# A transformer block on one core: the beginning dealt by a list schedule, with another form of the modulation

## The chip, the cores and the metric

The kernel runs on one core of a Trainium2 chip. The metric is the device time of one execution in microseconds (us). The engines are called as in the profile: PE is the matrix engine (PEld its weight loads), DVE the vector engine (VectorE), ACT the scalar engine, POOL is GpSimd, SP the engine that issues most loads and stores. Each runs its own queue in order; semaphores join them.

## What is computed

One block on x of 2048 tokens and 512 columns, all in float32: a modulated normalization, sliding-window attention of 32 heads with a window of 256, a gated residual, a second modulated normalization, a gated feed-forward part with 1792 inner columns, and a gated residual. All six modulation rows come from one vector c. Of the reference:

```python
mod = (_silu(c) @ w_mod).reshape(c.shape[0], 6, 1, -1)
sa, ca, ga, sb, cb, gb = (mod[:, 0], mod[:, 1], mod[:, 2], mod[:, 3], mod[:, 4], mod[:, 5])
h = _layernorm(x, axis=-1) * (1 + ca) + sa
x = x + ga * _A_ref(h, A_wqkv, A_wo)
h = _layernorm(x, axis=-1) * (1 + cb) + sb
x = x + gb * _B_ref(h, B_w1, B_w3, B_w2)
```

## The kernel before

Tokens are worked in four blocks of 512, each of four tiles of 128; the 512 columns are four quarters of 128. A float32 operand of a product is split into a high part, rounded to the fast matmul type (fp32r), and a low part; a product of two such operands is three matmuls.

The program has three phases. The **beginning** (all that this change touches) does this for each block: load four tiles of x, take mean and variance (`ln_tile`, L376 and L377), the root on POOL (L371), normalize on DVE (`ln_apply`, L381), then for each column quarter transpose four tiles on PE (L687), scale and shift on ACT with the modulation of that quarter (L388), split into high part (cast, L390) and low part (subtraction, L391), both on DVE. The result is `hT`. From it PE makes the values, twelve matmuls for each of 16 tiles (`values`, L709), evicted by ACT into `vS`, and, for the first group of heads, the queries and keys of blocks 0 to 2, twelve matmuls each (`unit_a`, L489). These are evicted three times by ACT (L495 to L501), two differences are made on POOL (`mix`, L507), and six loads lay them out in `ring`, whose constant rows POOL fills by memset (`ring_fill`, L460 to L463). For blocks 0 and 1 `unit_b` also runs the 16 score matmuls (L542) with the row maximum of each on DVE (L549). The weights of the values are split into `wvh` (ACT, L665) and `wvl` (L668: quarter 0 on POOL, the other three on DVE).

The **modulation** has six rows: for the first norm, j = 0 (shift) and 1 (scale); gates 2 and 5; for the second norm 3 and 4. Each row is loaded as four blocks of 256 KB into `stage`, which lies in the not yet used part of `vS`. PE multiplies silu(c), repeated over 32 columns, by the four blocks in four column groups of its array at once (L628), ACT evicts (L634), and a second set of matmuls sums the groups and turns the row into columns (L642) or, for the gates, into a row (L639) that is stored in `g_dr` and read much later.

The **middle** runs the attention of all other units by a table of times (`X`), and the **end** (second half of the attention's output, feed-forward) is dealt by `Sched`, a list schedule: operations with engine, price, key (the time wished), tiles read and written and PSUM banks are taken in the order in which a model clock frees their engine. Neither is touched.

In the beginning the order is written by hand: each operation is put down with a time by `at(t, fn)` with offsets from the table `W`, the whole list is sorted, and each engine's queue is that list, filtered. The values of a block are put down so that they run behind, among the transposes and projections of the block after it.

Of the kernel before, what the change touches and what calls it, by code (L numbers as in the profile page):

```python
# [8 lines left out]
F32 = mybir.dt.float32  # L9
# [34 lines left out]
W = dict(m=0.15, s=0.1, a=0.29, t=0.541, p=0.377, vs=1.762, vo=0.422, wq=(-1.8, 1.47, 1.5), wv0=-1.811, wvh=(-0.7, -0.65, -0.6, -0.55), wvl=(-0.5, -0.31, -0.3, -0.25), wp=1, A0=2.1, h0=0.539, h=6, hb=6.874, ls=3.287, la=1.146, rf=(1.55, 1.56, 8.4), v=2, vt=1.75, mr=(-1.85, 1.55), mm=(2.6, 4.625, 5.85, 9.2), ml=(-1.79, 1.25, 2.0, 4.9), A=1.268, At=7.876, B=10.4)  # L44
# [70 lines left out]
class Sched:  # L115
    def __init__(self, banks, take, fixed, urgent):


        self.ops, self.last, self.readers = [], {}, {}
        self.banks, self.take, self.fixed, self.urgent, self.tag = banks, take, fixed, urgent, None  # L120
        Bank.made = {}
# [33 lines left out]
    def deal(self):  # L155
# [20 lines left out]
        while left:  # L176
            best = None
            for e, lst in ready.items():
                t, pick = free[e], None
                for key, seq, o in lst:  # L180
# [10 lines left out]
                    if o.kb:  # L191

                        b = max(s, t)
                        end = max(wire, b + 1.5) + o.kb / RATE + o.more
                        s = max([s] + [u + 0.01 for u in self.urgent if b <= u < end])
                    if s <= t + (LOOK[e] if o.att else 0.0):
                        pick = (max(s, t), o)
                        break
# [35 lines left out]
            if o.kb:  # L234
                s = max(s, lanes.pop(0))
                wire = max(wire, s + 1.5) + o.kb / RATE + o.more
                o.lat = wire + LATE - s
# [43 lines left out]
def us(t):  # L281
# [8 lines left out]
             side_probs=("ACT", 0.48), values=("PE", 0.66), cut_all=("ACT", 0.48), store=("SP", 0.45))  # L290
NPE = 3
# [32 lines left out]
def block_kernel(ctx: ExitStack, tc: tile.TileContext, x, wqk, wv, wo, w13, w2, c, wmod, out):  # L324
# [11 lines left out]
    o32 = cst.tile([P, P], F32, name="o32")  # L336
    nc.gpsimd.memset(o32, 1.0 / 32)
    odd = cst.tile([P, 1], F32, name="odd")

    def fill_odd():  # L340
# [6 lines left out]
        nc.vector.tensor_copy(identr, ident)  # L347

    modc = cst.tile([P, 4, KC], F32, name="modc")
    sc32 = cst.tile([P, KC, 32], F32, name="sc32")  # L350
# [15 lines left out]

    def rstd_of(pool, mv, n, tag):
        var = pool.tile([P, n], F32, name=tag + "v")
        nc.vector.tensor_scalar_add(var, mv[:, :n, 1], EPS)
        rs = pool.tile([P, n], F32, name=tag + "r")  # L370
        nc.gpsimd.tensor_tensor(out=rs, in0=var, in1=nhalf[:, :n], op=ALU.pow)  # L371
        return rs

    def ln_tile(pool, xin, mv, i):
        st = pool.tile([P, nc.vector.BN_STATS_DIM], F32, name="bst", bufs=4)
        nc.vector.bn_stats(st, xin)  # L376
        nc.vector.bn_aggr(mv[:, i], st)  # L377

    def ln_apply(pool, xin, mv, rs, i, tag):
        xn = pool.tile([P, D], F32, name=tag, bufs=4) if tag else xin  # L380
        nc.vector.tensor_scalar(xn, xin, mv[:, i, 0:1], rs[:, i:i + 1], op0=ALU.subtract,  # L381
                                op1=ALU.mult)
        return xn

    def mod_split(pool, hT, src, k, lo, at):

        h = pool.tile([P, BT], F32, name="h32", bufs=3)
        nc.scalar.activation(h, src, AF.Identity, bias=modc[:, at, k:k + 1],  # L388
                             scale=modc[:, at + 1, k:k + 1])
        nc.vector.tensor_copy(hT[:, 0, k, lo:lo + BT], h)  # L390
        nc.vector.tensor_tensor(out=hT[:, 1, k, lo:lo + BT], in0=h,  # L391
                                in1=hT.bitcast(F32)[:, 0, k, lo:lo + BT], op=ALU.subtract)

# [26 lines left out]
    nc.gpsimd.memset(vS[:, :4, :, DH:], 1.0)  # L420

# [9 lines left out]
    def keys(rows, hh, a, b, n):  # L431
# [4 lines left out]
    nc.gpsimd.memset(mskq, 0.0)  # L436
    nc.gpsimd.affine_select(out=mskq[:, :P], in_=mskq[:, :P], pattern=[[1, P]], base=0,
                            channel_multiplier=-1, compare_op=ALU.is_gt, fill=NEG)
    nc.gpsimd.affine_select(out=mskq[:, 2 * P:], in_=mskq[:, 2 * P:], pattern=[[-1, P]], base=0,
                            channel_multiplier=1, compare_op=ALU.is_ge, fill=NEG)  # L440
    mskw = a1.tile([P, KC, P], F32, name="wqr", bufs=1)
    mskk = mskw[:, :2]
    nc.gpsimd.memset(mskk, 0.0)
    WIN = (dict(pattern=[[1, P]], base=0, channel_multiplier=-1, compare_op=ALU.is_ge, fill=NEG),
           dict(pattern=[[-1, P]], base=0, channel_multiplier=1, compare_op=ALU.is_gt, fill=NEG))
    for j in range(2):
        nc.gpsimd.affine_select(out=mskk[:, j], in_=mskk[:, j], **WIN[j])
# [4 lines left out]
    def fill_masks():  # L452
        nc.vector.tensor_copy(mskr, mskw[:, :2])
        nc.vector.tensor_scalar(later, mskw[:, 0], 0.0, None, op0=ALU.is_lt)
# [3 lines left out]
    def ring_fill(b, hh):  # L458
        k = ring.bitcast(F32)[:, 2 - 2 * hh, :, b * BT:(b + 1) * BT]
        nc.gpsimd.memset(k[:NM] if hh == 0 else k[:NS], 0.0)  # L460
        if hh:
            nc.gpsimd.memset(k[NS:NM], 1.0)
        nc.gpsimd.memset(k[NS:NS + 2], 1.0 - hh)  # L463
# [16 lines left out]
    def unit_a(u, t0, at, y=X):  # L480
# [35 lines left out]

        if b == 1 and g + 1 < NQ:
            for n in range(3):
                at(t0 + y["wqk"][n], lambda n=n: load_wqk(g + 1, n))
        for n in range(3 * KC):  # L520
            at(t0 + y["pj"][n], lambda n=n: product(n), "product")
        for n in range(3):
            at(t0 + y["ev"][n], lambda n=n: out(n), "out")
        at(t0 + y["mix"][0], lambda: mix(1), "mix")
        at(t0 + y["mix"][1], lambda: mix(2), "mix")
        for r in range(3):
            at(t0 + y["row"][r], lambda r=r: rows(r), "qk_rows")
# [1166 lines left out]
```

## Time and profile before

| what | us |
|---|---|
| median of 3 runs | 966.52 (965.93 to 967.31) |
| the profiled execution | 965.88, its span 963.9 |
| PE busy in the span | 938.2 (97%) |
| DVE, ACT, POOL busy | 720.3, 552.2, 524.9 |
| first matmul of the beginning | at 7.46 |
| first value product | at 19.93 |
| last value product, first operation of the middle | at 95.57, at 95.81 |

A row of the timeline gives the start, the duration, the engine, the source line, the operation with output and input tiles, the shapes and the count; in brackets the engine's idle time just before it and what ended it. Matmuls overlap, so what one costs is read from the distance between starts. The table by stretch gives busy microseconds of PE, PEld, DVE, ACT and POOL, with counts, then the granted PE clock, the DMA share and GB/s.

### The profile page before, as it was taken

To read this page: it belongs to the slowest core of one execution; us is meant where nothing else is said; L and a number is where in the kernel's file an instruction comes from. 1 tells how busy PE (TensorE), PEld (TensorE's weight loads), DVE (VectorE), ACT (ScalarE), POOL (GpSimd) and SP (SyncE) were. 2 spreads that over 40 slices of the span, in tenths; PEclk is the share of its full clock that TensorE was granted. 3 is DMA by queue.
4 is the path that set the end of the run, shared out by engine and by line. 5 is a ranking of instruction groups with operands and counts; after the bars stand their busy time and mean duration, and the time that the engine had idled before them with its cause. 6 is when DMAs were issued, how large, how long until landed. Compare 5 with 4: busy or idle time off the path is not lost.

```text
span 963.9 us, 17134 instructions
## 1 busy us (share of the span) xinstructions
PE 938.2 (97%) x5316; PEld 717.5 (74%) x5316; DVE 720.3 (75%) x2041; ACT 552.2 (57%) x1258; POOL 524.9 (54%) x734
## 2 busy tenths in 40 slices
PE   6999999999999999997999999999999999999998
PEld 3678777677777776774788778888888888888886
DVE  7575899898989898998568695666679665566545
ACT  3333877787878787875768944433456333433330
POOL 8321787777777777765643865368457332221320
PEclk9999999999999999998899999999999999999999
DMA  9521354444454444337692664575554523222002
GB/s 314 177 78 57 108 176 157 137 154 144 145 177 144 145 145 145 134 127 219 194 283 86 226 206 151 185 262 175 185 179 165 169 78 99 60 73 78 30 23 87
DMA packets 81559, 141.64 MB, mean 147 GB/s; under 512 B 10554, under 2 KB 23226, under 8 KB 81468
## 3 DMA queue, kind: packets, MB, share of 16 engines
q1 hardware_dynamic: 80748, 139.50, 44.6%
q10 hardware_dynamic: 720, 1.05, 0.3%
q8 instruction: 42, 0.69, 0.3%
q14 instruction: 49, 0.40, 0.1%
HBM read 85.72 MB, written 34.61 MB: 125 GB/s over the span
## 4 chain that ended last, share of the span: by engine, by line
PE 86%; DVE 4%; POOL 4%; DMA 2%; issue 2%; ACT 1%; SPq 0%; POOLq 0%; DVEq 0%; ACTq 0%
PE st L1469 11%; PE mx L1469 11%; PE pj L489 7%; PE mx L542 7%; PE st L819 7%; PE po L780 7%; PE mx L1563 6%; PE st L1563 6%; PE po L1469 4%; PE st L709 4%; PE pj L1469 3%; PE po L1563 2%; PE mx L1205 2%; PE pj L1563 2%; POOL pt L847 2%
## 5 line engine op out<-in xcount | busy, mean ns | idle before, releaser
L549 DVE CUSTOM_DVE_ANT_0 junk<-mx,mskq 128x384 bf16<-128x384 f32 (+2 forms) x503 | 251.9, 527 | 28.9 <-PE mx L542 27.5
L542 PE MATMUL mx<-ring 96*128 96x384 f32 (+1 forms) x503 | 151.9, 340 | 3.8 <-DMA ring<-qk 1.3
L819 PE MATMUL st<-ring 100*128 100x384 f32 (+2 forms) x488 | 148.7, 346 | 0.5 <-ACT pt L840 0.4
L847 POOL TENSOR_SCALAR_AFFINE_SELECT pt<-pt 128x256 f32<-128x256 f32 x268 | 108.6, 408 | 64.6 <-ACT pt L840 54.2
L489 PE MATMUL pj<-hT,wq 128*128 128x512 f32 x384 | 135.9, 404 | 0.8 <-DVE wq L478 0.8
L542 PEld LDWEIGHTS mx<-ring 96*128 96x128 f32 x503 | 92.2, 189 | 35.5 <-DVE mt L549 23.2
L1513 POOL TENSOR_TENSOR t<-t,t 128x512 f32<-128x512 f32 x28 | 41.0, 1463 | 137.6 <-DVE t L1501 133.8
L840 ACT ACTIVATE pt<-st 128x256 f32<-128x256 f32 x263 | 94.3, 386 | 36.2 <-DVE st L837 28.1
L819 PEld LDWEIGHTS st<-ring 100*128 100x128 f32 x488 | 91.7, 191 | 18.8 <-issue 6.7
L780 PE MATMUL po<-pt,vS 128*17 128x256 f32 (+2 forms) x1408 | 97.9, 390 | 2.3 <-POOL pt L847 1.8
L507 POOL TENSOR_TENSOR qk<-qkr,qk 128x512 fp32r<-128x512 f32 x64 | 83.3, 1301 | 27.6 <-ACT qkr L495 27.4
L837 DVE COPY_PREDICATED st<-later,st 128x128 f32<-128x128 uint8 x263 | 71.0, 291 | 13.4 <-PE st L819 10.6
L489 PEld LDWEIGHTS pj<-hT,wq 128*128 128x128 f32 x384 | 71.4, 190 | 9.6 <-issue 1.7
L1060 POOL TENSOR_TENSOR w<-w,w 128x512 fp32r<-128x512 f32 (+2 forms) x35 | 55.5, 1602 | 34.0 <-PE pj L1563 17.8
L780 PEld LDWEIGHTS po<-pt,vS 128*17 128x17 f32 x1408 | 32.8, 97 | 47.1 <-issue 21.0
L1501 DVE TENSOR_TENSOR t<-mx,t 128x512 f32<-128x512 f32 x54 | 36.9, 687 | 36.9 <-PE mx L1469 34.0
L1469 PE MATMUL st<-b,w 128*128 128x512 f32 x240 | 60.2, 390 | 1.4 <-ACT t L1508 1.4
L864 POOL TENSOR_SCALAR_AFFINE_SELECT sm<-sm 128x256 f32<-128x256 f32 x109 | 41.9, 406 | 28.4 <-ACT sm L854 24.3
L1469 PE MATMUL mx<-b,w 128*128 128x512 f32 x228 | 57.0, 391 | 0.0
L831 ACT ACTIVATE pt<-st 128x384 f32<-128x384 f32 (+2 forms) x109 | 45.7, 434 | 14.0 <-DVE st L827 12.5
L1469 PEld LDWEIGHTS st<-b,w 128*128 128x128 f32 x240 | 45.0, 188 | 11.4 <-ACT t L1508 1.8
L1501 DVE TENSOR_TENSOR t<-st,t 128x512 f32<-128x512 f32 x35 | 24.1, 688 | 37.1 <-PE st L1469 33.3
(322 smaller groups left out, 2097.0 us busy)
## 6 DMA issues: line engine op xcount, KB each, us to landing
ring<-qk SPq DMA_DIRECT2D x192, 128.0 KB
o_dr<-os SPq DMA_DIRECT2D x32, 256.0 KB
w<-wsum SPq DMA_DIRECT2D x14, 512.0 KB
w<-w2g SPq DMA_DIRECT2D x14, 512.0 KB
jb<-in_w SPq DMA_DIRECT2D x24, 256.0 KB
wraw<-in_w SPq DMA_DIRECT2D x7, 768.0 KB
w<-wraw SPq DMA_DIRECT2D x14, 384.0 KB
vS<-in_wmod SPq DMA_DIRECT2D x20, 256.0 KB
```

Source lines behind the costliest of these rows:

```text
L489: nc.tensor.matmul(v["ps"], WQ[g][w][:, n // 3], hTp(i, n // 3, b * BT, BT), start=(n == 0), stop=(n == 3 * KC - 1))
L507: nc.gpsimd.tensor_tensor(out=v[n], in0=v["raw"], in1=v[1].bitcast(F32), op=ALU.subtract)
L542: nc.tensor.matmul(v[i][:, :n], queries(NS, a, gq, 1), keys(NS, hh, a, k0, gq + 1 - k0), start=True, stop=True)
L549: nc.vector.tensor_tensor_reduce(out=junk[:, :n], in0=v[i][:, :n], in1=mskq[:, 3 * P - n:], scale=1.0, scalar=-3e38, op0=ALU.add, op1=ALU. ...
L780: nc.tensor.matmul(po[32 * i:32 * i + DH + 1, qb * P:(qb + nq) * P], vS[:, kb, 4 * g + i], pts[i // 2][:, i % 2, c0:c0 + nq], start=first, ...
L819: nc.tensor.matmul(ps[:, :nq], keys(NM, hh, a, kb, 1), queries(NM, a, kb, nq), start=True, stop=not plus)
L837: nc.vector.copy_predicated(ps[:, 0], later, ps[:, 2])
L840: nc.scalar.activation(pt_of(j, a)[:, hh, :2], v[j, a, hh][:, :2], AF.Exp, scale=SCALE)
L847: nc.gpsimd.affine_select(out=pt[:, :, 2 * m], in_=pt[:, :, 0], **w)
L1469: nc.tensor.matmul(ps(bk), WT[s, n][w][:, col], BB[t, k][r], start=start and c == 0, stop=stop and c == 5, skip_group_check=True)
L1501: return nc.vector.tensor_add(o, x, y)
L1563: nc.tensor.matmul(ps(bk), tiles[hk + (h,)][:, i * P:(i + 1) * P], w2_of(last, y, f), start=(m == 0), stop=(m == 5))
```

## The change

The beginning is no longer put down by hand. Every operation of it is entered by `do` or `dma` with its engine, price, key and the tiles that it reads and writes; `unit_a` and `unit_b` enter theirs through `at`; and `Sched` deals them, with the tables `K0` and `W0` of keys, its own DMA rate (`RATE0`) and look-ahead (`LOOK0`). [...]

Further:
- **First norm's modulation** (j = 0, 1): the weights are stored by column quarters. A quarter's four 128x128 blocks are stationary and a column of silu(c) moves (`mod_rows`), so that shift and scale of a quarter come out as columns at once (`mod_out`). Loads are interleaved: shift, scale and value weights of one quarter after the other.
- **Second norm's** (j = 3, 4): transposed weights, multiplied on DVE by silu(c), which is broadcast to all partitions (`crep`), and summed along the row (`mod_cols`), eight passes.
- **Gates** (j = 2, 5): each as one row, four accumulating matmuls with one column of silu(c) stationary (`gate_row`).
- All four `wvl` are made on POOL; two of the four first x tiles are loaded from ACT's queue; x has six buffers, by name; memsets of `ring` and masks become single operations; five matmuls on zeros stand first on PE.

```diff
+K0 = dict(wv=(7.0, 8.5), wl=1.0, h0=11.0, hb=19.0, tn=3.0, st=8.0, ap=4.0, mj=(22.0, 24.0), mg=(24.0, 40.0), rf=(13.0, 23.0, 40.0, 60.0),
+          va=3.0, pj=1.5, B=6.0, off=OFF0)
+RATE0, LATE0 = 390.0, 0.6
...
-        self.ops, self.last, self.readers = [], {}, {}
+        self.ops, self.last, self.readers, self.rate, self.late, self.look = [], {}, {}, RATE, LATE, LOOK
...
+    def apply(t):
+        nc.vector.tensor_scalar(xt[t], xt[t], mv[:, t, 0:1], rs[:, t // 4, 1, t % 4:t % 4 + 1],
+                                op0=ALU.subtract, op1=ALU.mult)
...
+    def mod_rows(j, n, bk):
+        w = stage[:, KC + KC * j + n].rearrange("p (k c) -> p k c", c=P)
+        for k in range(KC):
+            nc.tensor.matmul(ps(bk)[:, 2 * n + j:2 * n + j + 1], w[:, k], sc[:, k:k + 1], start=(k == 0),
+                             stop=(k == KC - 1))
+
+    def mod_out(n, bk):
+        nc.vector.tensor_tensor(out=modc[:, 0:2, n], in0=ps(bk)[:, 2 * n:2 * n + 2], in1=plus, op=ALU.add)
+
+
+    def mod_cols(j, n, i):
+        nc.vector.tensor_tensor_reduce(out=stage[:, i], in0=stage[:, i], in1=crep, scale=1.0, scalar=0.0,
+                                       op0=ALU.mult, op1=ALU.add, accum_out=modc[:, 2 + j, n:n + 1])
...
+    def gate_row(j, k, i, bk):
+        nc.tensor.matmul(ps(bk)[:1], sc[:, k:k + 1], stage[:, i], start=(k == 0), stop=(k == KC - 1))
...
+    for n in range(5):
+        bk = Bank("at")
+        do(0.5 + 0.1 * n, "PE", lambda bk=bk: nc.tensor.matmul(ps(bk)[:4], zero[:, 0], zero[:, 0, 0:1].to_broadcast([P, BT]),
+                                                                  start=True, stop=True), [], [bk], 0.46)
...
+        do(K0["wv"][1] + 2 * n, "POOL", lambda n=n: nc.gpsimd.tensor_tensor(
+            out=wvl[:, n], in0=stage[:, n], in1=wvh.bitcast(F32)[:, n], op=ALU.subtract), [("stg", n), ("wvh", n)],
+            [("wvl", n)], 1.24)
...
+        for n in range(5):
+            do(K0["rf"][b] + 1.0 * n, "POOL", lambda b=b, n=n: ring_fill(b, n), [], [("fill", b)], 1.0, port=False)
...
+            do(h - K0["ap"] + 0.46 * i + 0.5, "DVE", lambda t=t: apply(t), [q, ("rs", b)], [q], 0.46)
...
+            do(h - K0["tn"] + 1.3 * k + 1.5, "PE", lambda b=b, k=k, bk=bk: turn(b, k, bk), [
+                ("xt", (4 * b + i) % XS) for i in range(4)], [bk], 0.50)
+            do(h - K0["tn"] + 1.3 * k + 2.0, "ACT", lambda b=b, k=k, bk=bk: shifted(b, k, bk), [bk, ("mod", k)], [s_], 0.66)
+            do(h - K0["tn"] + 1.3 * k + 2.7, "DVE", lambda b=b, k=k: part(b, k, 0), [s_], [("hT", b, k, 0)], 0.46)
+            do(h - K0["tn"] + 1.3 * k + 3.2, "DVE", lambda b=b, k=k: part(b, k, 1), [s_, ("hT", b, k, 0)],
+               [("hT", b, k, 1)], 0.61, port=True)
...
+            do(K0["mg"][j] + 0.5 * k, "PE", lambda j=j, k=k, i=i, bk=bk: gate_row(j, k, i, bk), ["sc", ("stg", i)], [bk, ("gs", j, k)], 0.46)
...
+    sch = Sched([0.0] * 6 + [INF] * 2, take, [], [])
+    sch.rate, sch.late, sch.look = RATE0, LATE0, LOOK0
...
+    order = sch.deal()
```

Two places of the order. The first is POOL's queue behind the root of the first block, ahead of the first cast. `wvl` are the low parts of the value weights, `ring` rows are memsets. Before:

```order
L371 TENSOR_TENSOR rs0r<-rs0v,nhalf 128x4
L668 TENSOR_TENSOR wvl<-vS,wvh 128x512
L460 MEMSET ring 96x2x512
L462 MEMSET ring 4x2x512
L463 MEMSET ring 2x2x512
L460 MEMSET ring 100x2x512
```

And now:

```order
L631 TENSOR_TENSOR rs<-rs,nhalf 128x4
L723 TENSOR_TENSOR wvl<-vS,wvh 128x512
L451 MEMSET ring 100x2x512
L723 TENSOR_TENSOR wvl<-vS,wvh 128x512
L455 MEMSET ring 2x2x512
L723 TENSOR_TENSOR wvl<-vS,wvh 128x512
L451 MEMSET ring 96x2x512
L723 TENSOR_TENSOR wvl<-vS,wvh 128x512
```

The three subtractions that DVE made have moved to POOL, each between two memsets.

The second is PE's queue where block 1 follows block 0. L709 (now L655) are value products, L687 (now L639) transposes of a tile, L489 (now L481) projections, L537 scores, L680 gate products. Before:

```order
L709 MATMUL st<-wvl,hT 128x512
L687 MATMUL st<-ident,xt 128x128 x4
L709 MATMUL st<-wvh,hT 128x512 x2
L709 MATMUL st<-wvl,hT 128x512
L687 MATMUL st<-ident,xt 128x128 x4
L709 MATMUL st<-wvh,hT 128x512 x2
L709 MATMUL st<-wvl,hT 128x512
L709 MATMUL st<-wvh,hT 128x512
L687 MATMUL st<-ident,xt 128x128 x4
```

And now, the end of block 0's values:

```order
L655 MATMUL mx<-wvh,hT 128x512
L680 MATMUL mx<-vS,sc 1x512
L655 MATMUL mx<-wvh,hT 128x512
L655 MATMUL mx<-wvl,hT 128x512
L655 MATMUL mx<-wvh,hT 128x512
L680 MATMUL mx<-vS,sc 1x512 x3
L639 MATMUL st<-ident,xt_214 128x128
```

and, behind the last of 16 such transposes:

```order
L639 MATMUL mx<-ident,xt_330 128x128
L537 MATMUL mx<-ring 128x128 x2
L537 MATMUL st<-ring 128x128 x2
L481 MATMUL pj<-hT,wq_261 128x512
L537 MATMUL st<-ring 128x256
L481 MATMUL pj<-hT,wq_261 128x512
L481 MATMUL pj<-hT,wq_273 128x512
```

Block 0's values no longer lie among block 1's transposes; they come first, then all transposes of block 1, then products that read its `hT`. The same holds at the two later changes of block.

More of the change, by code (lines that the diff above doesn't have):

```diff
@@ L662, in load_wv, with turn, shifted, part @@
+    def turn(b, k, bk):
+        for i in range(4):
+            nc.tensor.transpose(ps(bk)[:, i * P:(i + 1) * P], xt[4 * b + i][:, k * P:(k + 1) * P], ident)
+    def shifted(b, k, bk):
+        hs[b, k] = p0.tile([P, BT], F32, name=f"h32{(KC * b + k) % 3}")
+        nc.scalar.activation(hs[b, k], ps(bk), AF.Identity, bias=modc[:, 0, k:k + 1], scale=modc[:, 1, k:k + 1])
+    def part(b, k, n):
+        lo = slice(b * BT, b * BT + BT)
         if n == 0:
[L663 to L668 removed]
@@ new lines, in block_kernel @@
+    do(9.0, "ACT", lambda: load_wqk(0, 1), *WQK(0, 1)[:2], 0.52)
+    do(9.5, "DVE", lambda: load_wqk(0, 2), *WQK(0, 2)[:2], 0.61)
+    for n in range(3):
+        do(2.0 + n, "POOL", lambda n=n: mask_k(n), [], ["qk2"], 0.29)
+        do(12.0 + n, "DVE", lambda n=n: fill_masks(n), ["qk2"] if n < 2 else [], [("later", n)], (0.3, 0.2, 0.2)[n])
+        do(30.0 + n, "POOL", lambda n=n: mask_q(n), [], ["mskq"], 0.35)
+    do(12.5, "DVE", fill_odd, [], ["odd"], 0.5)
+    do(11.0, "POOL", lambda: nc.gpsimd.memset(vS[:, :4, :, DH:], 1.0), [], ["ones"], 0.35, port=False)
@@ L763, in block_kernel @@
+    order = sch.deal()
+    if REPORT is not None:
+        REPORT(sch, sch.dealt)
     with tc.manual_schedule():
[L764 removed]
+        for fn in order:
             fn()
```

373 lines of the change are left out of this document (182 added, 191 removed).

## The prediction

> **What bounds the kernel now.** First the table of busy time by stretch, cut where PE starts the first value product (19.9) and where the next phase starts (95.8); then the chain that ended last.
>
> ```profile
> 0.00:19.90 19.90, 12.20 (x56) 5.09 (x56) 13.62 (x30) 7.92 (x15) 15.58 (x29) 1.00 0.91 318
> 19.90:95.80 75.90, 73.33 (x355) 54.80 (x355) 50.94 (x139) 27.20 (x50) 22.93 (x22) 1.00 0.35 115
> 95.80:963.90 868.10, 852.64 (x4907) 657.58 (x4905) 655.75 (x1874) 517.10 (x1194) 486.34 (x685) 0.99 0.45 146
> PE 86%; DVE 4%; POOL 4%; DMA 2%; issue 2%; ACT 1%; SPq 0%; POOLq 0%; DVEq 0%; ACTq 0%
> ```
>
> PE is the bound. The beginning, which alone changes, is its first 95.8 us; what follows keeps its order and only shifts. From 19.9 on PE rests 2.6 us in 76. So the change can win in two ways: PE's dense part starts sooner, or it holds less work. It can lose by new waits inside. The timeline of PE dates the start, the pace and the end:
>
> ```profile
> 7.46 5.81 PE L628 MATMUL mx<-vS,sc 128*32 128x512 f32 x16 [7.46 <-DVE sc L618]
> 19.93 0.50 PE L709 MATMUL st<-wvh,hT 128*128 128x512 f32 x1
> 22.93 0.50 PE L489 MATMUL pj<-hT,wq 128*128 128x512 f32 x1 [0.81 <-DVE wq L478]
> 23.50 0.95 PE L642 MATMUL mx<-o,h 128*128 128x1 f32 x8
> 93.23 0.39 PE L709 MATMUL st<-wvl,hT 128*128 128x512 f32 x1
> 95.33 0.40 PE L709 MATMUL st<-wvl,hT 128*128 128x512 f32 x1
> 95.81 0.86 PE L489 MATMUL pj<-hT,wq 128*128 128x512 f32 x3
> ```
>
> Nine products lie between 93.23 and 95.33: 0.233 us each. Of the 228 products (192 values, 36 projections) the timeline has eight, six of L709 and two of L489, between 19.93 and the wait that ends at 22.93, so the dense part starts in effect at 22.93 - 8 x 0.233 = **21.06**.
>
> **The work inside, before and after.** Prices are distances between starts:
>
> ```profile
> 27.98 1.06 PE L628 MATMUL mx<-vS,sc 128*32 128x512 f32 x8
> 28.98 0.50 PE L709 MATMUL st<-wvh,hT 128*128 128x512 f32 x1
> ...
> 34.77 0.47 PE L709 MATMUL st<-wvl,hT 128*128 128x512 f32 x1
> 35.17 1.05 PE L639 MATMUL mx<-h,o 128*32 128x512 f32 x2
> 36.15 0.50 PE L709 MATMUL st<-wvh,hT 128*128 128x512 f32 x1
> 36.48 0.40 PE L489 MATMUL pj<-hT,wq 128*128 128x512 f32 x1
> ...
> 37.18 0.60 PE L687 MATMUL st<-ident,xt 128*128 128x128 f32 x4
> 37.54 0.71 PE L709 MATMUL st<-wvh,hT 128*128 128x512 f32 x2
> 38.09 0.39 PE L709 MATMUL st<-wvl,hT 128*128 128x512 f32 x1
> ...
> 61.41 0.34 PE L542 MATMUL mx<-ring 96*128 96x384 f32 x1
> 61.59 0.63 PE L709 MATMUL st<-wvh,hT 128*128 128x512 f32 x2
> ```
>
> Common to both: 228 x 0.233 = 53.2; twelve groups of transposes at 0.36 and 0.09 for the switch, 5.4; scores (0.18 at 384 wide, in proportion below) 5.0. Sum 63.6.
>
> Before, after 22.93: three rows of modulation as four column groups (L628, 1.0), two turns (L642, 0.9) and two gate turns (L639: 36.48 - 34.77 less two products, 1.24): about 7.4. So 21.06 + 63.6 + 7.4 = 92.1, and 95.81 leaves 3.7 of waits.
>
> After: the first norm's modulation is done ahead; the second norm's goes to DVE (eight passes, off PE). Left are eight gate products. Each is a full-precision 512-wide matmul like L639's, one column instead of 32, which does not shorten the streaming of 512: 0.98 in a row, 1.24 alone. The order has one alone and three in a row, then two in a row and two alone: 1.24 + 3.20 + 2.22 + 2.48 = **9.1**, where the schedule books 0.46 each. PE gains no work time: +1.7. Bounds: 7.8 (all 0.98) to 9.9 (all 1.24).
>
> **The start.** Here the order on POOL and VectorE decides. Rows of both engines, and ACT's:
>
> ```profile
> 3.34 0.95 POOL L460 MEMSET ring<- 100x1024 f32 x1
> 3.43 1.01 DVE L453 CAST mskr<-wqr 128x256 fp32r<-128x256 f32 x1 [1.97 <-POOL wqr L447]
> 8.88 0.69 DVE L376 BATCH_NORM_STATS2 bst<-xt 128x6 f32<-128x512 f32 x1 [0.16 <-DMA xt<-in_x]
> 10.52 1.03 POOL L371 TENSOR_TENSOR rs0r<-rs0v,nhalf 128x4 f32<-128x4 f32 x1 [0.18 <-DVE rs0v L369]
> 11.59 1.92 DVE L381 TENSOR_SCALAR xt<-xt,mv,rs0r 128x512 f32<-128x512 f32 x4 [1.22 <-POOL rs0r L371]
> 14.56 1.28 POOL L668 TENSOR_TENSOR wvl<-vS,wvh 128x512 fp32r<-128x512 f32 x1 [3.01 <-ACT wvh L665]
> 15.93 2.11 ACT L388 ACTIVATE h<-st,modc 128x512 f32<-128x512 f32 x3
> 16.79 0.95 POOL L462 MEMSET ring<- 4x1024 f32 x1
> 17.51 0.51 DVE L390 CAST hT<-h 128x512 fp32r<-128x512 f32 x1
> 17.79 1.11 POOL L463 MEMSET ring<- 2x1024 f32 x1
> 18.05 0.69 DVE L391 TENSOR_TENSOR hT<-h,hT 128x512 fp32r<-128x512 f32 x1
> 18.66 0.53 DVE L390 CAST hT<-h 128x512 fp32r<-128x512 f32 x1
> ...
> L668 DVE TENSOR_TENSOR wvl<-vS,wvh x3: 680/680/1116, 15.3 to 16.9; 128x512 fp32r<-128x512 f32 x3
> ```
>
> Read the ends. The cast of 17.51 ends at 18.02, 0.28 after the memset that ends at 17.74; that of 18.66 ends at 19.19, 0.29 after the memset that ends at 18.90. The small cast of 3.43 takes 1.01 and also ends just behind a memset. So a one-input VectorE pass waits for the POOL instruction in progress, then runs 0.28; the memset queued meanwhile is held in turn (1.11 for 0.95). A two-input pass runs through a memset unharmed (0.69 at 18.05), but the first of VectorE's `wvl`, started beside POOL's `wvl`, took 1.12 for 0.68.
>
> [...]
>
> Before, POOL rested while the four tiles were normalized (11.59, four in 1.92). In the new order POOL's queue behind the root is product, memset, product, memset, and so on. Step by step, as an estimate from these rows: x is loaded ahead of all else, so statistics end nearer 9.1 than 9.8, and the root runs from 9.45 to 10.5, 1.1 earlier than before. In the normalization each tile then waits for one POOL instruction: 1.28 + 0.95 + 1.28 + 0.95 + 4 x 0.28 = 5.6 instead of 1.9; it ends at 16.1, against 13.5. Transposes end at 16.4, the first shifted block (ACT, 0.70 apart) at 17.2, behind 16.6 before. Its cast waits for the third `wvl`, 17.7; its low part ends at 18.4, the low part of the projection's weights at 19.15, and the second block's cast waits for the fourth `wvl`, 20.7. PE takes that block at 20.85 and is dense from there, with three products done: start in effect 20.85 - 0.7 = **20.15**, a gain of 0.9 only.
>
> Bounds: with no lock, normalization ends at 12.4, and the start is 17.8; with one POOL instruction more in the way, 21.4. I take 20.15, since all four casts before fit the lock.
>
> **The hand-overs between blocks.** Before, the transposes of a block lie among the values of the block ahead, which cover the way ACT, cast, low part. In the new order the values are used up first; then come four transposes in a row, and PE waits for that way. Prices, besides 0.70 and 0.28 above: a statistics pair 0.82, and 0.55 for the row maximum with its read-out of 0.08 (grouped lines):
>
> ```profile
> 22.79 0.69 DVE L376 BATCH_NORM_STATS2 bst<-xt 128x6 f32<-128x512 f32 x1
> 23.61 0.66 DVE L376 BATCH_NORM_STATS2 bst<-xt 128x6 f32<-128x512 f32 x1
> 37.53 0.43 DVE L390 CAST hT<-h 128x512 fp32r<-128x512 f32 x1 [5.01 <-ACT h L388]
> L549 DVE CUSTOM_DVE_ANT_0 junk<-mx,mskq 128x384 bf16<-128x384 f32 x24 | 12.7, 552 | 2.2 <-PE mx L542 2.2
> ```
>
> From the first to the second block: PE runs out at 20.85 + 57 x 0.233 + 4.4 = 38.6. By then VectorE has four statistics pairs and eight modulation passes behind it (two inputs and a read-out, about 0.70, held by POOL's two `mix` products); the root stands behind a memset, and the four normalizations interleave with four more memsets: 39.9. PE waits 1.3 for the last of them, then 1.3 for casts and low parts: 2.6. From the second to the third, seven row maxima (0.56 each) interleave with four casts and low parts (1.07 a pair); I count 8.4 us for PE's 7.2 of work: 1.2. From the third to the fourth, likewise, 1.3.
>
> That is 5.1 of waits where before had 3.7. Bounds: 2.5 (VectorE never late) and 8 (one us more at each).
>
> **The sum.** 20.15 + 63.6 + 9.1 + 5.1 = 98.0; two products of the next phase have slipped into the waits, -0.5: 97.5 against 95.8, **+1.7 us**. The profiled execution took 965.88 (span 963.9 and 2.0 around it), so 967.6; the median of the runs shown, 966.52, is 0.64 above it: **968.2**. What can be told from no change is about 0.2%, 1.9 us: 964.6 to 968.45.
>
> **Rivals.**
> The first: the start is won (chance 0.27). Place: the four normalizations. If POOL's products slip in without holding VectorE, the dense part starts 2.35 sooner and the second block's tiles are ready by 38.6: 968.2 - 2.35 - 1.3 = 964.6; with gates all at 0.98, 963.3. It decides if normalization ends before 13.0. For: before, four in 1.92. Against: POOL stood still then, and every lock row above.
> The second: PE goes slow after its rests (0.15). The rows of L628:
>
> ```profile
> L628 PE MATMUL mx<-vS,sc x48: 592/617/1062, 7.5 to 44.3; 128*32 128x512 f32 x48
> ```
>
> The earliest take 1062 ns, later ones 617. The change puts five idle products ahead, which warm PE, but leaves it about 3 us at rest before the transposes and over 1 us at each hand-over. If the slow pace returns once at the start (some 2 us of work at 1.7 times) and once later, it costs about 3: 971.2. Against: before, PE waited 0.8 us at 22 and kept its pace.
> The third: the broadcast of c arrives late (0.08). Its activation stands on ACT ahead of the third and fourth shifted blocks. At two us late the casts behind it move by 1.5: 969.7. No row shows such a load this early.
> [...]
>
> **How the numbers follow.** Forecast 0.50, its own range 966.3 to 970.6 from the bounds of the gates (-1.3, +0.8) and of one hand-over; of it 0.17 lies within 0.2%, 0.30 above, 0.03 below. The first rival gives 0.17 faster and 0.10 within; the second and third, 0.23 slower. Faster 0.20, same 0.27, slower 0.53. The range runs from the middle of the first rival, 964.0, to a little beyond the second, 972.
>
> **What would show it.** Normalization on VectorE: four rows stretched over 5 us with POOL's `wvl` between (right), or under 2.5 (the first rival). Second block's first projection near 20.9. Gate rows 0.98 apart. PE rests of 1 to 3 us just behind each later set of transposes. The next phase's first scores near 98 instead of 96.5. A start before 18.5 with hand-overs under 1 us each would prove me wrong; so would transposes or projections at 1.7 times their length (the second rival).

## The result, and the profile after

The changed kernel takes 963.92 us (median of 13 runs, 959.63 to 965.93); the kernel before took 966.55 on the same chip (13 runs, 964.81 to 968.72). The ratio is 0.997, 95% interval 0.9956 to 0.9984: faster by 0.3%, where 968.2, slower, was forecast. The profiled execution of the changed kernel took 960.54, its span 958.8.

First the table by stretch, for the kernel before, cut at the first value product, at the end of the last one, and at the first product of tile b with tile w, from where the end runs densely; its columns are those of the tables above:

```profile
0.00:19.93 19.93, 12.23 (x56) 5.09 (x57) 13.65 (x30) 7.95 (x15) 15.61 (x29) 1.00 0.91 318
19.93:95.80 75.87, 73.30 (x355) 54.80 (x355) 50.91 (x138) 27.17 (x50) 22.90 (x22) 1.00 0.35 115
95.80:521.20 425.40, 415.11 (x3003) 303.49 (x3002) 366.97 (x1469) 330.54 (x897) 299.08 (x527) 0.98 0.50 159
521.20:963.80 442.60, 437.53 (x1905) 354.08 (x1903) 288.78 (x406) 186.56 (x298) 187.27 (x158) 1.00 0.41 133
```

And for the changed kernel, cut at the same events:

```profile
0.00:24.08 24.08, 22.02 (x94) 16.09 (x95) 18.04 (x30) 7.40 (x12) 20.46 (x33) 0.73 0.92 316
24.08:98.25 74.17, 73.46 (x326) 53.26 (x325) 55.55 (x151) 25.82 (x42) 23.47 (x21) 1.00 0.30 97
98.25:521.80 423.55, 413.24 (x3001) 301.76 (x3000) 368.00 (x1470) 330.03 (x898) 299.08 (x527) 0.99 0.51 161
521.80:958.80 437.00, 431.47 (x1905) 354.45 (x1903) 288.63 (x406) 185.77 (x298) 188.57 (x158) 1.00 0.41 135
```

The beginning, all that the diff rewrites, ends at 98.25 instead of 95.80: **2.45 us later**. The gain lies behind it. The middle is 1.85 shorter, and the last row is **5.6 us shorter with the same 1905 matmuls**: up to the last 5.8 us PE rests no more than 1.5 us in either, the granted clock is 1.00, and still each product costs (442.6 - 437.0) / 1905 = 2.9 ns less. So +2.45 - 1.85 - 5.6 = -5.0, the difference of the two spans (963.9 and 958.8). The medians differ by 2.6 only: without the middle, which is taken up again at the end and is not the change's, +2.45 - 5.6 leaves -3.2.

What a product costs is the distance between starts. The timeline of PE in the end, the kernel before and then the changed one, the same products of w with wq:

```profile
723.55 2.96 PE L1563 MATMUL mx<-w,wq 128*128 128x512 f32 x12
726.35 1.56 PE L1563 MATMUL st<-w,wq 128*128 128x512 f32 x6
```

```profile
721.91 2.90 PE L1596 MATMUL mx<-w,wq 128*128 128x512 f32 x12
724.64 1.53 PE L1596 MATMUL st<-w,wq 128*128 128x512 f32 x6
```

From the first start to the second, 2.80 us for twelve, 233 ns each, have become 2.73, 227.5 each. Neither row waits for anything. Averaged over 550 to 950 us, b with o and b with wo went from 233.3 to 228.9, w with qk from 233.2 to 228.2, w with wq from 233.2 to 227.8; b with w hardly moved, 227.5 to 226.7.

One thing differs for these instructions: **where their tiles lie**. The diff drops two constants of 512 bytes per partition and adds one that takes 32:

```diff
-    o32 = cst.tile([P, P], F32, name="o32")
+    plus = cst.tile([P, 2], F32, name="plus")
-    sc32 = cst.tile([P, KC, 32], F32, name="sc32")
```

The pool `cst` lies at the bottom of the memory, and what is stacked on it, the tiles b, w and e of the end (pool `fp`) too, starts 992 bytes lower: b from byte 18304 of the partition to 17312. The tiles o, wo, qk and wq are allocated from the other side (`side="right"`) and did not follow: some buffers of qk and wq have other places, but modulo 256 bytes each lies as before. So the distance from a moving tile (b, w) to its stationary one (o, wo, qk, wq) has changed for most products of the end, and for b with w, both in `fp`, it has not.

### The profile page after: what moved, and what is told of

Read it like the earlier page. It is cut to its first block, busy times and chain, and to the rows that moved or that the text cites. A ratio compares the mean times of both kernels' runs of the same rounds, so it can differ in the third digit from the quotient of the medians.

```text
span 958.8 us, 17155 instructions
## 1 busy us (share of the span) xinstructions
PE 940.2 (98%) x5322; PEld 725.6 (76%) x5322; DVE 730.2 (76%) x2054; ACT 549.0 (57%) x1247; POOL 531.6 (55%) x738
## 4 chain that ended last, share of the span: by engine, by line
PE 83%; DVE 6%; POOL 4%; DMA 3%; issue 2%; ACT 1%; SPq 0%; ACTq 0%; POOLq 0%; DVEq 0%
PE st L1502 10%; PE mx L1502 9%; PE pj L481 7%; PE st L855 7%; PE mx L537 7%; PE po L816 7%; PE mx L1596 6%; PE st L1596 5%; PE po L1502 4%; PE mx L655 3%; PE pj L1502 2%; PE mx L1238 2%; PE st L655 2%; PE po L1596 2%; PE pj L1596 2%
## 5 line engine op out<-in xcount | busy, mean ns | idle before, releaser
L544 DVE CUSTOM_DVE_ANT_0 junk<-mx,mskq 128x384 bf16<-128x384 f32 (+2 forms) x487 | 244.0, 527 | 29.4 <-PE mx L537 27.9
L537 PE MATMUL mx<-ring 96*128 96x384 f32 (+1 forms) x487 | 146.0, 341 | 1.9 <-DMA ring<-qk 1.0
L481 PE MATMUL pj<-hT,wq 128*128 128x512 f32 x384 | 133.9, 407 | 0.0
L537 PEld LDWEIGHTS mx<-ring 96*128 96x128 f32 x487 | 88.8, 189 | 32.4 <-DVE mt L544 21.7
L481 PEld LDWEIGHTS pj<-hT,wq 128*128 128x128 f32 x384 | 71.6, 191 | 7.2 <-DVE hT L650 0.7
L1502 PEld LDWEIGHTS st<-b,w 128*128 128x128 f32 x240 | 45.0, 188 | 10.9 <-ACT t L1541 1.5
```

The source lines that it names most:

```text
L481: nc.tensor.matmul(v["ps"], WQ[g][w][:, n // 3], hTp(i, n // 3, b * BT, BT), start=(n == 0), stop=(n == 3 * KC - 1))
L537: nc.tensor.matmul(v[i][:, :n], queries(NS, a, gq, 1), keys(NS, hh, a, k0, gq + 1 - k0), start=True, stop=True)
L544: nc.vector.tensor_tensor_reduce(out=junk[:, :n], in0=v[i][:, :n], in1=mskq[:, 3 * P - n:], scale=1.0, scalar=-3e38, op0=ALU.add, op1=ALU. ...
L1502: nc.tensor.matmul(ps(bk), WT[s, n][w][:, col], BB[t, k][r], start=start and c == 0, stop=stop and c == 5, skip_group_check=True)
```

## The experiments

Three theories. *Address*: the pace of a product depends on where its two tiles lie. *Order*: the new beginning leaves other banks, queues or buffers to what follows. *Pace*: the profiled execution was quick by chance. An unused tile in `fp` moves the end's tiles and nothing else:

```diff
             pools["fp"] = fp
+            fp.tile([P, 8], F32, name="pad")
```

**First set**: 8 columns (32 bytes) in the kernel before and in the changed one, 16 (64 bytes) in the changed one, 24 (96 bytes) in the kernel before.

> The kernel before with one unused tile of 32 bytes per partition ahead of the tiles of the end, so that their first byte moves from 0 to 32 modulo 64, as it lies in the changed kernel. Instructions and their order are the same. Address theory (a 512-wide product is slower where the moving tile and the next stationary tile lie differently modulo 64): the products of the gated feed-forward part, 550 to 950 us, fall from about 231.5 ns apart to about 228, and those on tiles that disagreed from 233 to 229; 1240 products x 4 to 5 ns make the kernel 5 to 6 us faster, about 961. Order theory (the gain comes from the new beginning: other banks, queues or buffers for what follows): no change, 966.5. Pace theory (the profiled execution of the changed kernel ran at a quicker pace by chance): 231.5 stays, no change.

> The changed kernel with the same unused tile of 32 bytes, so that the tiles of the end go back to 0 modulo 64. Address theory: the products of the end return to about 233 apart where the tiles disagree, and the kernel loses 5 to 6 us: 969 to 970, slower than the kernel before by about 0.3%, near what was forecast of the new beginning alone. Order theory and pace theory: no change, about 964.

> The changed kernel with 64 unused bytes: the tiles of the end at 32 modulo 64 as in the changed kernel, but at 96 modulo 128, where their partners lie. Address theory in its plain form (modulo 64 alone): no change, 964. In a finer form (agreeing modulo 128 saves more: the trace of the changed kernel has 229 ns for pairs at 32 and 96, 227 for pairs at 32 and 32): another 860 products x 2 ns, 2 us faster, 962. If a pad of any size disturbs the end, it is slower.

> The kernel before with 96 unused bytes: the tiles of the end at 96 modulo 128, as their partners. Address theory, plain form: as with 32 bytes, about 961. Finer form: another 2 us, about 959, faster than the changed kernel by 0.5%. Order theory and pace theory: 966.5.

Measured, with the ratio to the kernel before on the same chip (966.44): e1 960.89, 0.9947 (0.993 to 0.9964); e2 967.37, 1.0016 (1.0003 to 1.0029); e3 966.73, 1.0008 (0.9992 to 1.0023); e4 964.62, 0.9985 (0.997 to 1.0). Of each kernel the row from 550 to 950 us in the table by stretch, in the order before, changed, e1, e2, e3, e4; the number behind PE's busy time counts the matmuls done in 400 us:

```profile
550.00:950.00 400.00, 400.00 (x1735) 323.70 (x1734) 264.63 (x363) 160.56 (x254) 169.18 (x146) 1.00 0.40 130
```

```profile
550.00:950.00 400.00, 399.64 (x1760) 328.65 (x1760) 267.81 (x367) 160.37 (x254) 170.80 (x146) 1.00 0.41 132
```

```profile
550.00:950.00 400.00, 399.67 (x1760) 328.74 (x1759) 266.65 (x366) 160.07 (x253) 168.37 (x144) 1.00 0.41 132
```

```profile
550.00:950.00 400.00, 400.00 (x1737) 324.49 (x1736) 265.11 (x363) 161.43 (x255) 169.71 (x147) 1.00 0.40 131
```

```profile
550.00:950.00 400.00, 399.94 (x1739) 324.99 (x1739) 265.35 (x363) 161.05 (x254) 169.72 (x147) 1.00 0.40 131
```

```profile
550.00:950.00 400.00, 399.96 (x1739) 325.08 (x1738) 265.16 (x363) 162.16 (x256) 171.05 (x147) 1.00 0.40 131
```

32 unused bytes give the old kernel the whole pace of the new one (1760) and take it from the new one (1737). The median of e2 lost 3.4 us of the 5 to 6 that were expected, though in its profile the end takes 442.3. That rules out order and pace, and address is left. But the form of the theory fell: with the tiles at 96 modulo 128 (e3 and e4) the plain form wanted the quick pace of 1760 and the finer one 2 us more, and both kernels came out near the slow pace instead (1739). Agreement modulo 64 is not the rule.

**Second set**: the distance, by moving the partners, and the beginning by itself.

> The kernel before with 32 unused bytes per partition on the other side of the memory: the tiles of the end that are multiplied (b, w) stay at 0 modulo 128, their stationary partners o and wo move from 96 to 64, qk and wq stay at 96. Distance theory (what counts is the distance of the two tiles; 64 bytes apart modulo 128 is the good one, as with 32 against 96): products of b with o and wo fall from 233.3 to 229 ns, those of w with qk and wq stay at 233; 580 products x 4 ns, 2.4 us faster, 964. Place theory (the moving tile itself has to lie at 32 modulo 128): all stay at 233, 966.5.

```diff
     a1 = ctx.enter_context(tc.tile_pool(name="a1", bufs=1, side="right", reuse_waits="tile"))
+    a1.tile([P, 8], F32, name="pad")
```

Measured: 964.97, ratio 0.9969 (0.9952 to 0.9985). b with o and wo fell to 229.1 and 229.4 ns though b stayed where it was; w with qk and wq stayed at 233.0 and 233.2. It is the **distance** of the two tiles.

> The changed kernel with 992 unused bytes ahead of the tiles of the end, so that each of them has exactly the address that it has in the kernel before; what is left of the change is the new beginning. Address theory: the products of the end return to the kernel before's 231.5 on average, and the time is the kernel before's plus the new beginning alone, +1 to +3 us: 967.5 to 969.5. If something else in the change quickens what follows: 964.

Measured (the pad has 248 columns): 967.35, ratio 0.9992 (0.9975 to 1.0009). Every group of the end is back at the old kernel's pace within 0.1 ns (b with o 233.3, w with qk 233.3, w with wq 233.2), and the end takes 442.75. The time is a miss: the kernel before took 967.8 on this chip, 1 to 3 us more than that was expected, and it came out 0.45 below, though the beginning ends at 98.89. The twelve runs spread from 965.1 to 971.2, and what the beginning alone costs needed a better pair, the last one below.

Grouped by the distance modulo 256, the products so far fell into classes: 0 near 227 ns, 192 near 229, 32, 128, 160 and 224 near 233. That gave the next test, where the largest classes get distance 0, and one class the untried 64 (the pad has 56 columns):

> The kernel before with 224 unused bytes ahead of the tiles of the end: the distance from the moving tile to the next stationary one, modulo 256, becomes 0 for b with o and wo and for w with qk, qkr and half of wq (it was 224 before, 192 in the changed kernel), and 64 for the other half of wq, a distance that no run has had yet. Distance theory modulo 256 (all runs so far grouped by it: 0 gives 227.4 ns, 192 gives 229.1, and 32, 128, 160 and 224 give 233): products of b with o fall from 233.3 to 227, and the end takes 435 to 436 us where it took 442.6 before and 437.0 in the changed kernel: 959 to 960, faster than the kernel before by 0.7%. Rival (192 is the one good distance): 233 stays, 966.5.

Measured: 959.37, ratio 0.9943 (0.9921 to 0.9964); b with o 226.7, w with qk 227.0. Distance 0 is better than 192, as expected. The half of wq at distance 64 stayed slow, at 232.0, where the changed kernel has 227.8 for w with wq, so the end takes 436.5, not 435 to 436.

**The beginning's own terms.** The lock (VectorE's one-input pass waited for the POOL instruction in progress: in the changed kernel the first tile's normalization took 2.37 us and ended 0.27 behind a memset) and PE's clock, on the changed kernel:

> The changed kernel with three of the four value low parts back on VectorE, behind the normalization, and with three memsets of the ring moved behind the first block's casts: POOL has one instruction instead of seven beside normalization and first cast. Lock theory: normalization ends at about 12.4 instead of 16.3, the first transposes then stand behind PE's modulation products, which end at 15.1; the first block is ready 1.2 us sooner, and the kernel is 1 us faster, 963. Clock theory (at the start PE's half clock is the bound, the lock only beside it): the dense part still starts near 23.5, within 0.6 us of before.

```diff
-        do(K0["wv"][1] + 2 * n, "POOL", lambda n=n: nc.gpsimd.tensor_tensor(
+        low.append(lambda n=n: (nc.vector if n else nc.gpsimd).tensor_tensor(
...
     order = sch.deal()
+    for fn in low[1:]:
+        if order.index(fn) < order.index(scales[3]):
+            order.remove(fn)
+            order.insert(order.index(scales[3]) + 1, fn)
+    for fn in fills[5:8]:
+        order.remove(fn)
+    spot = order.index(cast[3]) + 1
+    order[spot:spot] = fills[5:8]
```

`scales[3]` is the last normalization of block 0, `cast[3]` its last cast, `fills[5:8]` the first three memsets of block 1. Measured: 961.41, ratio 0.9926 (0.9902 to 0.995). VectorE's and POOL's rows of that run:

```profile
9.47 1.49 DVE L635 TENSOR_SCALAR xt<-xt,mv,rs 128x512 f32<-128x512 f32 x1 [1.22 <-POOL rs L632]
10.95 3.53 DVE L635 TENSOR_SCALAR xt<-xt,mv,rs 128x512 f32<-128x512 f32 x3
...
9.40 1.27 POOL L724 TENSOR_TENSOR wvl<-vS,wvh 128x512 fp32r<-128x512 f32 x1
10.73 1.11 POOL L453 MEMSET ring<- 4x1024 f32 x1
11.90 1.11 POOL L455 MEMSET ring<- 2x1024 f32 x1
13.07 1.12 POOL L451 MEMSET ring<- 100x1024 f32 x1
```

Half a test only: with nothing to wait for, POOL ran the next memsets at once, and each tile waits for one of them, 1.2 us a tile where four took 1.92 in the kernel before. Normalization ends at 14.5, not 12.4, against 16.3. Still the first value product comes at 22.79 instead of 24.08 and the beginning ends at 96.73, 1.5 sooner: that much of the loss this run took away. How much of it is the lock's is open: PE's half clock is shorter here too, 10.24 us (12.2 to 22.5) instead of the changed kernel's 13.65. (The medians gained more, 0.9926 against 0.997, on another chip; the rest is not explained.)

> The changed kernel with six more products on zeros, 256 columns each, one behind each of the first six modulation products of PE, in its idle time before the first transposes. Clock theory: PE's granted clock stays whole between 10.9 and 24.6 us, four transposes take 0.55 instead of 1.09 and eight modulation rows 0.95 instead of 1.71, and the dense part starts about 2 us sooner: 962. If a third of the time is too little to hold the clock: half clock as before, and the fillers delay the first transposes by about 1 us: 965.

```diff
+    idle = psA.tile([P, BT], F32, name="pj", bufs=1)
+    for fn in mods[:6]:
+        order.insert(order.index(fn) + 1, lambda: nc.tensor.matmul(
+            idle[:4, :256], zero[:, 0], zero[:, 0, 0:1].to_broadcast([P, 256]), start=True, stop=True))
```

Measured: 966.46, ratio 0.9992 (0.9975 to 1.0009), above the changed kernel's 0.997, though the two intervals overlap; the beginning ends at 103.14, 4.9 later. PE's rows:

```profile
10.84 1.05 PE L665 MATMUL st<-sc,vS 128*128 128x1 f32 x8
11.82 0.60 PE L800 MATMUL pj<-zero 128*4 128x256 f32 x2
12.35 1.63 PE L665 MATMUL st<-sc,vS 128*128 128x1 f32 x8
...
20.33 1.11 PE L639 MATMUL st<-ident,xt 128*128 128x128 f32 x4
```

The second outcome: about a third of the time in wide products (0.53 of 1.51 us) did not hold the clock. It halves all the same, at 12.6, eight rows go from 1.05 to 1.63, and the fillers delay the first transposes by 4 us (the fourth starts at 16.34 in the changed kernel, the first here at 20.33), more than the expected 1.

> The changed kernel with its five products on zeros cut from 512 columns to 4, so that nothing warms PE at the start. Clock theory: the whole start runs at half clock until the dense part; the modulation products before 10.9 us, which ran at 0.12 us a row, take 0.18, some 1 us later; the beginning ends 0.5 to 1.5 us later, at 99 to 99.7, and the time is 965. If the loads of the modulation weights bound the start: no change, 964. If the warm-up only brings the slow stretch forward (the clock is lowered when a warm PE does little): the clock is whole later on, transposes at 0.55 instead of 1.09, and the beginning ends 1 us sooner, 963.

```diff
-        do(... nc.tensor.matmul(ps(bk)[:4], zero[:, 0], zero[:, 0, 0:1].to_broadcast([P, BT]),
+        do(... nc.tensor.matmul(ps(bk)[:4, :4], zero[:, 0], zero[:, 0, 0:1].to_broadcast([P, 4]),
```

Measured: 964.48, ratio 0.999 (0.9974 to 1.0006). PE's rows:

```profile
7.93 3.54 PE L665 MATMUL mx<-sc,vS 128*128 128x1 f32 x16 [6.43 <-DMA vS<-in_wmod]
11.34 6.97 PE L665 MATMUL st<-sc,vS 128*128 128x1 f32 x32
18.17 1.09 PE L639 MATMUL st<-ident,xt 128*128 128x128 f32 x4
```

Sixteen rows take 3.54 where they took 1.92, and the beginning ends at 100.19, 1.9 later than in the changed kernel: the clock theory, a little beyond its range. The half pace is read from the rows: the profile of this run records no clock before 25.85. By the profiles the warm-up earns its place, and does not bring the slow stretch on; the medians' intervals overlap (0.999 against 0.997).

**Last**, both gains together, and a pair with all distances at 0.

> The changed kernel with the low parts of the value weights back on VectorE and the memsets moved, as in the run without most of the lock, and with 192 unused bytes, which makes the distances of the end 0 modulo 256. If both gains are real and add up: the beginning ends near 96.7 instead of 98.2, the end takes 435 to 436: 960 or a little below, faster than the kernel before by 0.7% to 0.9%. If the distance 192 was already the best: 961.5.

Measured: 962.21, ratio 0.9962 (0.9946 to 0.9977). A miss: the beginning ends at 97.23, the end takes 436.4 (the half of wq at distance 64 again), and the time lies above that of e7, whose interval it overlaps by a hair (0.9946 to 0.995). The two gains were not shown to add up.

> The kernel before with 192 unused bytes between the tiles of the other side and 32 ahead of the tiles of the end, so that every moving and every stationary tile of the end lies at 160 modulo 256: all distances 0. Distance theory: also w with the second half of wq, which stood at 231.8 ns with 224 bytes, falls to 227: 335 products x 5 ns, 1.7 us; the end takes 434.5 to 435.5 us (442.6 before, 437.0 in the changed kernel), the kernel about 958, 0.8% faster than before. Rival (a tile's own place decides, not the distance): some group stays above 229, the end at 436 or more.

```diff
                 v["mt"] = a1.tile([P, 2, 2, 4], F32, name=f"mt{u % 2}", bufs=1)
+                if u == 0:
+                    a1.tile([P, 48], F32, name="gap")
...
             pools["fp"] = fp
+            fp.tile([P, 8], F32, name="pad")
```

> The changed kernel with the same distances, all 0; what tells it from the kernel before with all distances 0, on the same chip, is the new beginning alone. By the profiles (the beginning ends at 95.6 to 96.6 us with the old one, at 98.2 to 98.9 with the new): the end as short as there, 434.5 to 435.5, and the kernel 2 to 2.5 us slower than that one, 960 to 961. If the new beginning gives its loss back in the middle (two products of the middle are done in it): less than 1 us apart.

(The changed kernel needs the gap alone.) Measured: e12 957.87, ratio 0.9919 (0.99 to 0.9938); e13 961.16, ratio 0.9955 (0.9937 to 0.9972). The last stretch of e12, then of e13:

```profile
522.70:957.30 434.60, 428.93 (x1905) 354.33 (x1903) 288.69 (x406) 185.96 (x298) 187.10 (x158) 1.00 0.42 135
```

```profile
522.83:957.60 434.77, 428.97 (x1905) 354.43 (x1903) 288.41 (x406) 185.62 (x298) 187.65 (x158) 1.00 0.41 135
```

And the products of w with wq in e12:

```profile
722.31 2.88 PE L1566 MATMUL mx<-w,wq 128*128 128x512 f32 x12
725.03 1.52 PE L1566 MATMUL st<-w,wq 128*128 128x512 f32 x6
```

226.7 ns each, and every larger group of the end is between 226.6 and 226.8. The same 1905 matmuls take 434.6 where the kernel before needed 442.6. **The old beginning with the tiles in place has the lowest time of all, 0.8% below the kernel before** (e7's interval, 0.9902 to 0.995, overlaps it), and with the end alike the new beginning is 3.3 us slower than the old one (961.16 against 957.87; their intervals against the kernel before just touch at 0.9937).

All fifteen profiled executions together, products from 550 to 950 us, by the distance from the moving tile to the next product's stationary tile, modulo 256 bytes (the few long gaps left out):

| distance | mean ns between starts | kernels | means of the kernels | products |
|---|---|---|---|---|
| 0 | 227.1 | 15 | 226.7 to 227.6 | 13061 |
| 192 | 229.1 | 8 | 228.9 to 230.7 | 6178 |
| 64 | 232.0 | 2 | 232.0 | 333 |
| 128 | 233.0 | 2 | 233.0 | 2112 |
| 32 | 233.1 | 3 | 233.0 to 233.1 | 480 |
| 224 | 233.2 | 4 | 231.2 to 233.4 | 2722 |
| 160 | 233.4 | 1 | 233.4 | 1055 |

The rows 32 and 64 are mixtures. Where a product's own stationary tile lies at the same distance as the next one's, 32 gives 230.1 (320 products) and 64 gives 233.3 (222); 160 products whose own distance is 224 and the next one's 32 take 239.0. So the next tile's distance is not all that counts.

## Why the prediction was wrong, and where it was right

**The step that failed** is the one taken for granted: "The beginning, which alone changes, is its first 95.8 us; what follows keeps its order and only shifts." It keeps its order, and its addresses moved by 992 bytes; most products of the end went from distance 224 to 192. That is worth 5.6 us in the profiles (442.6 to 437.0) and 3.4 to 5.6 in the medians (e2 against the changed kernel, e1 against the kernel before). No rival had it, and no row of the profile before could show it as a cost, because a PE that is busy throughout looks alike at 227 and 233 ns. What was within reach: the diff removes tiles from a pool on which everything else stands, and in the old trace the products of b with w were already quicker than those of b with o.

**The beginning** was forecast 1.7 us slower. It is: 2.45 in the two profiles and 3.3 in the medians of e13 and e12 (2.9 in their profiles), though not in the medians of e6. The end of the beginning, forecast at 98.0 before the credit for two products slipped in, came at 98.25. But two terms were off, against each other.

- *The lock was right.* Forecast: normalization from 10.5 to 16.1, a POOL instruction ahead of each tile. VectorE's and POOL's rows of the changed kernel:

```profile
9.93 2.37 DVE L634 TENSOR_SCALAR xt<-xt,mv,rs 128x512 f32<-128x512 f32 x1 [1.22 <-POOL rs L631]
12.29 3.99 DVE L634 TENSOR_SCALAR xt<-xt,mv,rs 128x512 f32<-128x512 f32 x3
...
17.66 0.43 DVE L648 CAST hT<-h 128x512 fp32r<-128x512 f32 x1 [1.24 <-ACT h L643]
...
20.81 0.16 DVE L669 TENSOR_TENSOR modc<-mx,plus 128x2 f32<-128x2 f32 x1 [0.31 <-PE mx L665]
20.88 0.42 DVE L648 CAST hT<-h 128x512 fp32r<-128x512 f32 x1
...
9.86 1.27 POOL L723 TENSOR_TENSOR wvl<-vS,wvh 128x512 fp32r<-128x512 f32 x1
11.07 0.96 POOL L451 MEMSET ring<- 100x1024 f32 x1
11.98 1.45 POOL L723 TENSOR_TENSOR wvl<-vS,wvh 128x512 fp32r<-128x512 f32 x1
13.48 1.11 POOL L455 MEMSET ring<- 2x1024 f32 x1
...
18.23 1.72 POOL L723 TENSOR_TENSOR wvl<-vS,wvh 128x512 fp32r<-128x512 f32 x1 [1.06 <-ACT wvh L721]
```

  It ended at 16.28: it began 0.6 sooner, and its first tile waited for two of POOL's instructions (it ended at 12.30, 0.27 after the memset that ends at 12.03), the others for one each. The first cast came at 17.66 (forecast 17.7). The second came at 20.88 (20.7), but the agreement is luck: the fourth `wvl` had ended at 19.95, and the cast stood behind `mod_out` (L669), which waited for PE's modulation rows. The first rival, a start without the lock, is out.
- *The start was mis-sized*: effective start 20.15 forecast; the first value product comes at 24.08 with four projection products done, 24.08 - 4 x 0.233 = 23.15, **3.0 late**. "PE takes that block at 20.85 and is dense from there" failed. PE went slow, as in the second rival, at this one place, but not after a rest: its clock fell in the midst of the modulation rows. PE's rows, then two rows of the table by stretch:

```profile
7.53 1.92 PE L665 MATMUL mx<-sc,vS 128*128 128x1 f32 x16 [0.49 <-DMA vS<-in_wmod]
9.52 5.69 PE L665 MATMUL st<-sc,vS 128*128 128x1 f32 x32
...
18.18 1.09 PE L639 MATMUL mx<-ident,xt 128*128 128x128 f32 x4
19.06 1.71 PE L665 MATMUL mx<-sc,vS 128*128 128x1 f32 x8
20.63 1.09 PE L639 MATMUL mx<-ident,xt 128*128 128x128 f32 x4
...
22.80 1.05 PE L639 MATMUL st<-ident,xt 128*128 128x128 f32 x4
```

```profile
4.10:10.90 6.80, 6.23 (x36) 3.71 (x34) 4.28 (x11) 0.75 (x2) 5.24 (x6) 1.00 1.01 376
10.90:24.55 13.65, 13.26 (x59) 12.27 (x59) 11.44 (x15) 5.63 (x9) 12.28 (x13) 0.50 0.99 343
```

  Sixteen rows in 1.92 are 0.12 each, the later ones 0.2. From 10.9 to 24.6 PE's clock is granted at half (0.73 on average in the first row of the table above). A quarter's rows and transposes then take 2.45 us (from 18.18 to 20.63), and PE, not VectorE, sets the step from block to block.
- *Gates*: 9.1 forecast, 7.3 measured, 0.95 alone and 0.89 each for three in a row:

```profile
36.72 1.02 PE L680 MATMUL mx<-vS,sc 128*1 128x512 f32 x2
37.67 0.50 PE L655 MATMUL mx<-wvh,hT 128*128 128x512 f32 x1
...
38.57 2.74 PE L680 MATMUL mx<-vS,sc 128*1 128x512 f32 x6
41.23 1.53 PE L639 MATMUL st<-ident,xt 128*128 128x128 f32 x12
```

  Each product has two records, of 590 to 592 ns with one stationary column, where those of the old kernel's L639 with 32 took 592 to 617. They follow closer than those did (0.98 in a row, 1.24 alone). Forecast right in kind, 1.8 too high.
- *Hand-overs*: 5.1 of waits forecast; PE is idle 0.7 us between 19.9 and 98.25, its one wait above 0.2 us being 0.47, for a row maximum. What is left, 98.25 - 23.15 - 63.6 - 7.3 = 4.2, is nearly all work that takes longer than assumed: values at 0.240 us instead of 0.233 (1.3), projections at 0.26 (0.9), scores 6.8 with that wait instead of 5.0 (1.8), and two products of the middle (0.5), less 0.3 for transposes that took 5.1 instead of 5.4.

So the sum came out because a start 3.0 late met 1.8 less for the gates and waits that were not there. "Transposes or projections at 1.7 times their length" was named as what would prove the forecast wrong, and did show, at the start only.

**The middle**, 1.85 shorter in these two executions, is not the change's. Near 444 us PE waits (2.27 us ahead of 444.02 in the changed kernel) and its clock drops for a while; the rows there, of the kernel before, then the changed one:

```profile
440.00:450.00 10.00, 7.94 (x48) 4.39 (x48) 7.12 (x26) 2.95 (x8) 2.76 (x8) 0.68 0.79 240
```

```profile
440.00:450.00 10.00, 7.63 (x51) 3.90 (x50) 7.46 (x31) 4.21 (x14) 3.62 (x9) 0.83 0.70 217
```

The half clock there lasts 3.4, 6.8 or 10.2 us in the fifteen executions, and the stretch from the beginning's end to the first product of b with w takes 423.6 to 424.7, 425.4, and 426.5 to 427.9 with it, with either beginning. That is much of the spread between runs of one kernel: of the changed kernel's 13, the seven with a mean granted clock of 0.984 took 963.9 to 965.9, the four with 0.988, the profiled one among them, 960.5 to 963.8.

## What to carry to other kernels

When an edit adds or drops tiles, compare the addresses of the tiles that untouched matmuls read, and look at the distance between starts in the untouched stretch of both traces, before the difference in time is put down to the edit. In the end of this kernel, where PE hardly ever waits, a few unused bytes that bring moving and stationary tiles to a distance of 0 modulo 256 were worth more here (8 us of 966) than the change itself. And before a small product is given to PE for being small, look in the trace at what PE's clock does behind it: here 128x1 rows were followed by 13.65 us at half clock.

## What the hardware showed unexpectedly

In the end of this kernel a 512-wide product in fp32r cost 226.7 ns (e12) or 233.3 (b with o, the kernel before) according to the distance of the moving and the stationary tile, 0 or 224 bytes modulo 256; at 192, 228.9 (the changed kernel), it lies between. By the order theory and the pace theory a pad would change nothing, and the runs disagree by 6.6 ns a product. Why the distance counts, and whether it is the product's own stationary tile or the next one's, is open: the two lie alike nearly everywhere, and where they differ neither alone explains the pace. It isn't all, either: in the middle the projections (hT with wq) have a median of 233 or 234 ns at the distances 0 and 64 in both kernels and at 32 in the kernel before, and why is open too.

Products that keep PE busy by the profile did not keep its clock: in the changed kernel 128x1 rows back to back from 7.53 to 10.9 us were followed by half clock (0.50 from 10.9 to 24.55), in e8, with wide fillers for a third of the time, by half clock from 12.6; and without a warm-up (e11) 10.24 us of them without a gap (7.93 to 18.17) did not end the half pace, the last 32 rows taking 0.21 us each like the first 16. The slow stretches that the traces record last 13.653 us at the start of the changed kernel, 3.413 and 6.827 between 443 and 465 us in it and in the kernel before, 10.24 at the start of e7 and 17.067 in e8; no run shows what sets these lengths.
